# A decode step on one core: K cache turned by half units instead of quarters, with fewer VectorE instructions around it

## The chip, the core and the metric

The kernel runs on one core of a Trainium2 chip. The core has engines that run side by side: TensorE (PE, matmuls; PEld is its weight load), VectorE (DVE), ScalarE (ACT), GpSimd (POOL) and SyncE (SP), which here only issues DMAs. They order themselves by semaphores. The metric is the device time of one execution in microseconds, lower is better; the time before is a median of three runs.

## What is computed

Two sequences (B = 2) take one decode step each. A gate g = sigmoid(sum(x * gate_w)) mixes an attention block over a cache with a small dense block:

```
q = (x @ wq)                      x: 2 x 512, wq: 512 x 4096 (32 heads of 128)
p = softmax(q . K / sqrt(128))    K, V: 2 x 32 heads x 4096 keys x 128, bf16
a = (p . V) @ wo                  wo: 4096 x 512
b = relu(x @ w1) @ w2             w1: 512 x 1376, w2: 1376 x 512
out = g * a + (1 - g) * b
```

K and V are 67 MB each; everything else together is about 11 MB.

## The kernel before, in words

**Storage.** K and V are each cut into 8 units of 8 heads (8.39 MB, 64 KB on each of 128 partitions). Three regions of SBUF (`kv[:, 0..2]`) hold units in turn. The order of units is written out by hand: k0 to k4, then v0, k5, v1, k6, v2, k7, then v3 to v7. Unit n goes to region n mod 3, and after v7 the region of v5 takes wo and w2. wq, w1, x, gate_w and a 128x128 identity lie in region 2 at first, ahead of k2.

**DMA.** SP issues all large loads in that order from one queue (lines 216 to 239). Ahead of each it waits on the semaphore that says that the unit which last used the region is read: `pe_sc_u` for a K unit (its last score matmul), `pe_v_u` for a V unit. k2 instead waits for `pe_h`, `dve_setup` and `dve_q`, since it overwrites the small weights. ACT issues the two tiny loads of x and gate_w.

**Opening.** POOL builds constants (`constants`). `gate` turns x and gate_w by PE, copies them out of PSUM by VectorE, multiplies and sums them there, and spreads the sum to all partitions by a float32 matmul with ones; ACT takes the exponent, VectorE finishes g and 1 - g. `setup` reduces the identity to several masks. `q_proj` makes q, VectorE turns it into `q_sb`, and ACT writes it into the weight tiles `wz` (`w_block`). `ffn_h` makes h on PE in 11 blocks of w1's columns (the last of 96), and four VectorE instructions apply ReLU and the factor 1 - g.

**A K unit.** The keys land as rows. `k_turn` (L360) transposes the region in place on VectorE in 32x32 blocks of 32-bit words, in four instructions of 4096 words per partition. `k_scores` then runs 64 matmuls of 512 columns on PE, 16 for each of these quarters; of each four only the first loads weights (L393), the other three keep them (L365, a helper's line). The first matmul of a quarter waits for its turn `dve_kt_u_rp`. Scores of a whole batch (four K units) gather in four PSUM banks.

**Softmax.** After k3 (batch 0) and k7 (batch 1): `sm_max` on VectorE (maximum, then small turns), `sm_exp` on ACT, `sm_turn` on VectorE (turns the exponents E). `spread` on POOL multiplies E with a mask into the weights `ptm` for one V unit. `o_denominator` sums the exponents by four tiny matmuls and takes the reciprocal on VectorE.

**A V unit.** `v_unit`: 64 matmuls of 512 columns. `v_extract`: two VectorE instructions (L455, L459) reduce the result. `v_gather`: a small matmul adds it to the unit's batch.

**Order of work.** Each engine runs its list in the order in which the program adds to it (end of the kernel function): k0 to k3, softmax of batch 0, k4, then for v = 0 to 2 the V unit followed by one K unit, softmax of batch 1 after k7, and the rest of the V units. VectorE's list is thus: turns of k0 to k3, `sm_max(0)`, `sm_turn(0)`, turns of k4, extract of v0, turns of k5, and so on. At the end `o_scale`, `o_place`, and `project`, in which wo and w2 are multiplied as they land; VectorE and ACT cast the result and SP stores it.

Of the kernel before, what the change touches and what calls it, by code (L numbers as in the profile page):

```python
# [4 lines left out]
ALU = mybir.AluOpType  # L5
# [79 lines left out]
def bass_gated_mix__gqa_block_cached__dense_activation_relu__decode_kernel(  # L85
# [22 lines left out]
    id2 = sb("id2", [2, 2], bf16)  # L108
    xT = sb("xT", [128, 4, 2], bf16)
    xT32 = sb("xT32", [128, 4, 32], bf16)  # L110
    gwT = sb("gwT", [128, 4], bf16)
    xg = sb("xg", [128, 4, 2], f32)
    xgs = sb("xgs", [128, 2], f32)
# [27 lines left out]
    x_sb = kv[0:2, C, 21888:22400]  # L141
    gw_sb = kv[0:1, C, 22400:22912]
    ident = kv[:, C, 22912:23168].bitcast(f32)
    ones = kv[:, C, 23168:23424].bitcast(f32)
# [69 lines left out]
    act(lambda e: e.dma_start(x_sb, A_x.rearrange("b s d -> (b s) d")).then_inc(sem["x"], 16))  # L214
    act(lambda e: e.dma_start(gw_sb, gate_w.rearrange("(o d) -> o d", o=1)).then_inc(sem["gw"], 16))
# [20 lines left out]
    sp(lambda e: e.dma_start(w2_sb[0:96, 10, :], B_w2[1280:1376, :]).then_inc(sem["w2a"], 16))  # L236
    W2 = (("w2b", 0, 5, 0), ("w2c", 640, 4, 5), ("w2d", 1152, 1, 9))
    for name, row, n, r0 in W2:
        sp(lambda e, name=name, row=row, n=n, r0=r0: e.dma_start(
            w2_sb[:, r0:r0 + n, :].rearrange("p r n -> p (r n)"),  # L240
            B_w2[row:row + 128 * n, :].rearrange("(p r) n -> p (r n)", p=128)).then_inc(sem[name], 16))
# [4 lines left out]
    def constants():  # L246
        pool(lambda g: g.memset(id2[:], 0.0), signal="c_idz")
        pool(lambda g: g.affine_select(out=id2[:], in_=id2[:], pattern=[[-1, 2]], compare_op=ALU.not_equal, fill=1.0,
                                       base=0, channel_multiplier=1), waits=["c_idz"], signal="c_id2")
        pool(lambda g: g.memset(ones, 1.0), signal="c_ones")  # L250
        pool(lambda g: g.memset(ident, 0.0), signal="c_i0")
        pool(lambda g: g.affine_select(out=ident, in_=ident, pattern=[[-1, 128]], compare_op=ALU.not_equal, fill=1.0,
                                       base=0, channel_multiplier=1), waits=["c_i0"], signal="c_ident")
        pool(lambda g: g.memset(xT32[:], 0.0), signal="c_x32")
        for i in range(2):
            pool(lambda g, i=i: g.memset(wz[:, i], 0.0), signal=("c_wz" if i else None))
        pool(lambda g: g.memset(mpad[:], 0.0), signal="c_mpad")
        pool(lambda g: g.memset(selx[:], 0.0), signal="c_selx")
        for i in range(2):
            pool(lambda g, i=i: g.memset(sell[:, i], 0.0), signal=("c_sell" if i else None))  # L260
        pool(lambda g: g.memset(srow[:], 0.0), signal="c_s0")
        pool(lambda g: g.affine_select(out=srow[:], in_=srow[:], pattern=[[-1, 263]], compare_op=ALU.not_equal, fill=1.0,
                                       base=7, channel_multiplier=8), waits=["c_s0"], signal="c_srow")

    def setup():
        dve(lambda v: v.tensor_reduce(out=maskc[:], in_=ident.rearrange("p (t c h) -> p c t h", t=4, c=4), axis=AX.XY, op=ALU.add),
            waits=["c_ident"])
        dve(lambda v: v.tensor_reduce(out=mmax[:], in_=ident.rearrange("p (h x) -> p h x", h=8), axis=AX.X, op=ALU.add),
            signal="dve_m8")
        dve(lambda v: v.tensor_copy(out=mask8[:], in_=mmax[:]), waits=["dve_m8"], signal="dve_mask8")  # L270
# [8 lines left out]
    def gate():  # L279
        for t in range(4):  # L280
            pe(lambda e, t=t: e.transpose(PSB[0:128, XT_B0 + 2 * t:XT_B0 + 2 * t + 2], x_sb[:, t::4], id2[0:2, 0:2]),
               waits=(["c_id2"] if t == 0 else []), dwaits=([(sem["x"], 16)] if t == 0 else []))
        for t in range(4):
            pe(lambda e, t=t: e.transpose(PSB[0:128, XT_B0 + 8 + 2 * t:XT_B0 + 9 + 2 * t], gw_sb[:, t::4], id2[0:1, 0:1]),  # L284
               dwaits=([(sem["gw"], 16)] if t == 0 else []), signal=("pe_xT" if t == 3 else None))
        dve(lambda v: v.tensor_copy(out=xT[:], in_=PSB[0:128, XT_B0:XT_B0 + 8].rearrange("p (t b) -> p t b", t=4)),  # L286
            waits=["pe_xT"], signal="dve_xT0")
        dve(lambda v: v.tensor_copy(out=xT32[:, :, 0:2], in_=PSB[0:128, XT_B0:XT_B0 + 8].rearrange("p (t b) -> p t b", t=4)),
            waits=["c_x32"], signal="dve_x32")
        dve(lambda v: v.tensor_copy(out=gwT[:], in_=PSB[0:128, XT_B0 + 8:XT_B0 + 16:2]), signal="dve_xT")  # L290
        dve(lambda v: v.tensor_tensor(out=xg[:], in0=xT[:], in1=gwT[:].unsqueeze(2).to_broadcast([128, 4, 2]), op=ALU.mult),
            waits=["dve_xT"], signal="dve_xg")
        dve(lambda v: v.tensor_reduce(out=xgs[:], in_=xg[:].rearrange("p t b -> p b t"), axis=AX.X, op=ALU.add),
            waits=["dve_xg"], signal="dve_xgs")
        pe(lambda e: e.matmul(psf(0, 128, G_C0, 2), lhsT=ones, rhs=xgs[:, :], start=True, stop=True),
           waits=["dve_xgs", "c_ones"], signal="pe_z")
# [10 lines left out]
    def q_proj():  # L307
        wqv = wq_sb.rearrange("p (t u a x) -> p t a u x", t=4, u=4, a=4)
        for half in range(2):
            for t in range(4):  # L310
                for a in range(4):
                    pe(lambda e, half=half, t=t, a=a: e.matmul(  # L312
                        psf(32 * a, 32 * a + 32, V_C0 + BANK * half, BANK), lhsT=xT32[:, t, :],
                        rhs=wqv[:, t, a, 2 * half:2 * half + 2, :], start=(t == 0), stop=(t == 3), tile_position=(0, 32 * a)),
                       dwaits=([(sem["wq"], 16)] if half == 0 and t == 0 and a == 0 else []),
                       waits=(["dve_xT0", "dve_x32"] if half == 0 and t == 0 and a == 0 else []),
                       signal=("pe_q" if half == 1 and t == 3 and a == 3 else None))
# [8 lines left out]
    def ffn_h():  # L326
        for ft in range(11):
            m = 128 if ft < 10 else 96
            for t in range(4):
                def fn(e, ft=ft, t=t, m=m):  # L330
                    o = t * DFF
                    cols = w1_sb[:, o + 1280:o + 1376]
                    for _, row, n, r0 in W2:
                        if r0 <= ft < r0 + n:
                            cols = w1_sb[:, o + row + ft - r0:o + row + 128 * n:n]
                    return e.matmul(psf(0, m, H_C0 + 2 * ft, 2), lhsT=cols, rhs=xT[:, t, :], start=(t == 0), stop=(t == 3))
                pe(fn, dwaits=([(sem["w1"], 16)] if ft == 0 and t == 0 else []),
                   signal=("pe_h" if ft == 10 and t == 3 else None))
        for b in range(2):
            dve(lambda v, b=b: v.tensor_scalar(out=hT[:, 0:10, b], in0=PSF[:, H_C0 + b:H_C0 + 20:2], scalar1=0.0,  # L340
                                               scalar2=gm[:, b:b + 1], op0=ALU.max, op1=ALU.mult),
                waits=["pe_h", "dve_gm"])
            dve(lambda v, b=b: v.tensor_scalar(out=hT[0:96, 10, b:b + 1], in0=psf(0, 96, H_C0 + 20 + b, 1), scalar1=0.0,
                                               scalar2=gm[0:96, b:b + 1], op0=ALU.max, op1=ALU.mult),
                signal=f"dve_h{b}")
# [10 lines left out]
    def k_turn(u):  # L356
        what = ("k", u)
        reg = kv[:, reg_of(what), :].bitcast(dt.uint32)
        for rp in range(4):
            dve(lambda v, rp=rp: v.transpose(out=reg[:, 4096 * rp:4096 * (rp + 1)], in_=reg[:, 4096 * rp:4096 * (rp + 1)]),  # L360
                dwaits=([landed(what)] if rp == 0 else []), signal=f"dve_kt_{u}_{rp}")
# [8 lines left out]
    def k_scores(u):  # L370
        b, ub = divmod(u, 4)
        keys = kv[:, reg_of(("k", u)), :].rearrange("p (r j q e) -> p r j q e", j=2, q=32, e=2)
        for rp in range(4):
            pos = 8 * ub + 2 * rp
            for blk in range(4):
                j, e_ = divmod(blk, 2)
                for rb in range(4):
                    rc = 4 * rp + rb
                    waits = []
                    if blk == 0 and rb == 0:  # L380
                        waits = [f"dve_kt_{u}_{rp}"]
# [16 lines left out]
    def sm_max(b):  # L398
        dve(lambda v: v.tensor_reduce(out=mpad[:, 0:2], in_=PSF[:, 0:2048].rearrange("p (x h q) -> p h x q", h=2, q=16),  # L399
                                      axis=AX.XY, op=ALU.max),  # L400
            waits=[f"pe_sc_{4 * b + 3}", "c_mpad"] + ([f"dve_mt{b - 1}"] if b else []), signal=f"dve_m{b}")
# [51 lines left out]
    def v_extract(v):  # L453
# [4 lines left out]
            waits=[f"pe_v_{v}"] + ([f"dve_y_{v - 1}"] if v else []), signal=f"dve_x_{v}")  # L458
        dve(lambda e: e.tensor_reduce(out=X3[:], in_=X2[:].rearrange("p (c d) -> p d c", c=4), axis=AX.X, op=ALU.add),  # L459
            waits=[f"dve_x_{v}"] + ([f"pe_g_{v - 1}"] if v else []), signal=f"dve_y_{v}")  # L460
# [7 lines left out]
    def o_denominator(b):  # L468
        for h in range(2):
            pe(lambda e, h=h: e.matmul(psf(0, 32, L_C0 + b, 1), lhsT=sell[:, h, :], rhs=lsum[:, b, h:h + 1],  # L470
                                       start=(h == 0), stop=(h == 1), skip_group_check=True),
               waits=([f"act_exp{b}", "dve_setup", "dve_h1"] if h == 0 else []), signal=(f"pe_l{b}" if h else None))
        dve(lambda v: v.reciprocal(out=rinv[:, b:b + 1], in_=psf(0, 32, L_C0 + b, 1)), waits=[f"pe_l{b}"], signal=f"dve_rinv{b}")

    def o_scale(b):
        dve(lambda v: v.tensor_scalar(out=O_sb[:, b, :], in0=psf(0, 32, O_C0, 128), scalar1=rinv[:, b:b + 1],
                                      scalar2=gb[0:32, b:b + 1], op0=ALU.mult, op1=ALU.mult),
            waits=[f"pe_g_{4 * b + 3}", f"dve_rinv{b}", "dve_g"], signal=f"dve_O{b}")
# [54 lines left out]
    o_denominator(0)  # L533
    w_block(6)
    for v in range(8):
        v_unit(v)
        v_extract(v)
# [13 lines left out]
        if v == 3:  # L551
            o_denominator(1)
# [37 lines left out]
```

## Time and profile before

| quantity | value |
|---|---|
| time, median of 3 runs | 344.62 us (344.28 to 344.64) |
| the profiled execution's own time | 344.46 us |
| its span, first to last instruction | 343.1 us |
| busy: PE / VectorE / ACT / POOL | 179.8 / 169.7 / 13.5 / 35.5 us |
| mean granted TensorE clock | 0.781 of full speed |
| read from HBM | 145.43 MB, 424 GB/s over the span |
| VectorE's K turns (L360) | 32, 139.3 us in all, 4.41 us each |
| score matmuls (L393 and L365) | 128 and 384, 52.9 and 114.0 us |

How to read it: busy times are of one execution; engines overlap, so they don't add up to the span. A row of the time line gives start, duration, engine, line and operation, and in brackets the idle time ahead of it with what ended it. A busy PE counts pipelined matmuls, so its share says little of its speed; the granted clock (0.50 or 1.00 in most windows) says how fast it could go. DMA share above 1.0 in a short window is an effect of how packets are stamped.

### The profile page before, as it was taken

What the parts mean: (1) busy time and instruction counts of PE and PEld (TensorE: products, weight loads), DVE (VectorE), ACT (ScalarE), POOL (GpSimd) and SP (SyncE); (2) the same over time, 40 slices, a digit from 0 to 9 for tenths busy, and PEclk for the clock granted to TensorE, in tenths of its full rate; (3) what the DMA queues carried; (4) which work ended last, traced back from release to release, by engine and by line L of the source; (5) the groups of instructions that cost most, each with busy time, mean ns of one, the idle gap of its engine ahead of it and who ended that gap; (6) DMA issues with size and microseconds to landing.
All of it is one profiled execution on the core that took longest, in us unless ns stands there. A gap on an engine that the chain in (4) does not pass through costs nothing.

```text
span 343.1 us, 2541 instructions
## 1 busy us (share of the span) xinstructions
PE 179.8 (52%) x1322; PEld 39.6 (12%) x938; DVE 169.7 (49%) x87; ACT 13.5 (4%) x44; POOL 35.5 (10%) x50
## 2 busy tenths in 40 slices
PE   0510196996869409935980099205970503307353
PEld 0210000100001000120120011100020201102122
DVE  0210797979899489439910694219935020102020
ACT  1010001000010110000000000000020000000000
POOL 3000000000000040040013000400004040403100
PEclk9965599899989957995995579955996575856586
DMA  8998989999999989898999989999999999999995
GB/s 325 451 483 374 481 374 481 397 458 420 435 460 390 489 382 474 382 468 390 466 466 391 481 384 466 405 451 405 460 405 443 466 392 474 413 401 449 395 428 216
DMA packets 3588, 145.59 MB, mean 424 GB/s; under 512 B 405, under 2 KB 634, under 8 KB 890
## 3 DMA queue, kind: packets, MB, share of 16 engines
q1 hardware_dynamic: 3572, 145.43, 98.5%
q8 instruction: 9, 0.15, 0.2%
q10 hardware_dynamic: 6, 0.00, 0.0%
q14 instruction: 1, 0.01, 0.0%
HBM read 145.43 MB, written 0.00 MB: 424 GB/s over the span
## 4 chain that ended last, share of the span: by engine, by line
DMA 57%; DVE 24%; PE 9%; issue 4%; another core or an unknown queue 3%; SPq 1%; ACT 1%
DMA kv<-in_A_k_cache_dram 34%; DVE kv L360 22%; DMA kv<-in_B_w_dram 13%; DMA kv<-in_A_v_cache_dram 11%; PE PS L365 4%; PE PS L448 4%; PE PS L393 2%; DVE E L422 1%; ACT E L414 1%; DVE mpad L399 1%; DVE X L459 0%; SPq L232 0%; DVE X L455 0%; PE PS L500 0%
## 5 line engine op out<-in xcount | busy, mean ns | idle before, releaser
L360 DVE STREAM_TRANSPOSE kv<-kv 128x4096 uint32<-128x4096 uint32 x32 | 139.3, 4412 | 50.2 <-DMA kv<-in_A_k_cache_dram 50.2
L365 PE MATMUL PS<-kv,wz 128*128 128x512 bf16 x384 | 114.0, 407 | 0.0
L393 PE MATMUL PS<-kv,wz 128*128 128x512 bf16 x128 | 52.9, 413 | 94.5 <-DVE kv L360 94.4
L431 POOL TENSOR_TENSOR ptm<-E,mask 128x512 bf16<-128x512 bf16 x32 | 32.2, 1039 | 282.2 <-DVE E L422 158.5
L448 PE MATMUL PS<-kv,ptm 128*32 128x512 bf16 x512 | 38.6, 462 | 36.3 <-DMA kv<-in_A_v_cache_dram 36.3
L455 DVE TENSOR_TENSOR X<-PS,maskc 128x512 f32<-128x512 f32 x8 | 5.5, 687 | 79.4 <-PE PS L448 79.4
L393 PEld LDWEIGHTS PS<-kv,wz 128*128 128x128 bf16 x128 | 13.0, 102 | 206.2 <-DVE kv L360 120.6
L448 PEld LDWEIGHTS PS<-kv,ptm 128*32 128x32 bf16 x512 | 17.5, 113 | 54.3 <-issue 47.2
L351 ACT ACTIVATE wz<-q_sb 32x8 bf16<-32x8 bf16 x32 | 6.9, 214 | 154.5 <-PE PS L365 145.6
L464 PE MATMUL PS<-X,selx 128*32 128x128 f32 x16 | 3.5, 302 | 13.3 <-DVE X L459 13.3
L459 DVE TENSOR_REDUCE X<-X 128x128 f32<-128x512 f32 x8 | 8.2, 1024 | 0.3
L399 DVE TENSOR_REDUCE mpad<-PS 128x2 f32<-128x2048 f32 x2 | 4.6, 2292 | 7.5 <-PE PS L365 7.5
L414 ACT ACTIVATE E<-PS,negm 128x1024 bf16<-128x1024 f32 x4 | 4.4, 1109 | 81.8 <-DVE negm L410 81.8
L422 DVE STREAM_TRANSPOSE E<-E 128x2048 bf16<-128x2048 bf16 x2 | 4.6, 2312 | 4.7 <-ACT E L414 4.7
L312 PE MATMUL PS<-kv,xT 128*32 128x512 bf16 x32 | 3.6, 629 | 3.6 <-DMA kv<-in_A_wq_dram 3.6
L500 PE MATMUL PS<-kv,oW 128*2 128x128 bf16 x128 | 2.9, 264 | 4.5 <-DMA kv<-in_A_wo_dram 4.5
L510 DVE CAST ptm<-PS 2x128 bf16<-2x128 f32 x2 | 0.6, 280 | 9.1 <-PE PS L500 9.1
L319 DVE STREAM_TRANSPOSE ptm<-PS 128x1024 f32<-128x1024 f32 x1 | 1.3, 1251 | 6.3 <-PE PS L312 6.3
L286 DVE COPY xT<-PS 128x8 bf16<-128x8 bf16 x1 | 0.2, 164 | 8.1 <-PE PS L284 8.1
L510 ACT ACTIVATE ptm<-PS 2x128 bf16<-2x128 f32 x2 | 0.5, 270 | 84.0 <-PE PS L500 84.0
L464 PEld LDWEIGHTS PS<-X,selx 128*32 128x32 f32 x16 | 1.1, 112 | 19.0 <-DVE X L459 15.7
L500 PEld LDWEIGHTS PS<-kv,oW 128*2 128x2 bf16 x128 | 2.5, 102 | 4.8 <-DMA kv<-in_A_wo_dram 4.2
(56 smaller groups left out, 24.2 us busy)
## 6 DMA issues: line engine op xcount, KB each, us to landing
kv<-in_A_v_cache_dram SPq DMA_DIRECT2D x1, 6144.0 KB, 47.8
kv<-in_A_wq_dram SPq DMA_DIRECT2D x1, 4096.0 KB, 12.2
kv<-in_A_wo_dram SPq DMA_DIRECT2D x2, 2048.0 KB, 40.1
kv<-in_A_v_cache_dram SPq DMA_DIRECT2D x1, 2048.0 KB, 52.3
kv<-in_B_w_dram SPq DMA_DIRECT2D x1, 1376.0 KB, 15.0
kv<-in_B_w_dram SPq DMA_DIRECT2D x1, 640.0 KB, 43.4
kv<-in_B_w_dram SPq DMA_DIRECT2D x1, 512.0 KB, 44.2
kv<-in_A_k_cache_dram SPq DMA_DIRECT2D x8, 40.2
```

The source lines that it names most:

```text
L351: act(lambda e, a=a: e.activation(out=wz[32 * a:32 * a + 32, u % 2, :, 31 + 32 * a:33 + 32 * a], in_=q_sb[32 * a:32 * a + 32, b, ub].rearr ...
L360: dve(lambda v, rp=rp: v.transpose(out=reg[:, 4096 * rp:4096 * (rp + 1)], in_=reg[:, 4096 * rp:4096 * (rp + 1)]), dwaits=([landed(what)] i ...
L365: return e.add_instruction(mybir.InstMatmult(name=nc.get_next_instruction_name(), engine=mybir.EngineType.PE, ins=[e.lower_ap(rhs), e.lowe ...
L393: return e.matmul(dst, lhsT=w, rhs=m, start=first, stop=final, skip_group_check=True)
L399: dve(lambda v: v.tensor_reduce(out=mpad[:, 0:2], in_=PSF[:, 0:2048].rearrange("p (x h q) -> p h x q", h=2, q=16), axis=AX.XY, op=ALU.max) ...
L414: act(lambda a, h=h: a.activation(out=E[:].rearrange("p (x h q) -> p h x q", h=2, q=16)[:, h], in_=PSF[:, 0:2048].rearrange("p (x h q) -> ...
L422: dve(lambda v: v.transpose(out=E[:], in_=E[:]), waits=[f"act_exp{b}"], signal=f"dve_et{b}")
L431: pool(lambda g, src=src, dst=dst: g.tensor_tensor(out=dst, in0=src, in1=msk, op=ALU.mult), waits=([f"dve_et{b}", "dve_mask8"] + ([f"pe_v_ ...
L448: pe(lambda e, ci=ci, t=t: e.matmul(psf(32 * t, 32 * t + 32, c0, 512), lhsT=ptm[:, ci].rearrange("p c h -> p (c h)"), rhs=rows[:, 512 * ci ...
L455: dve(lambda e: e.tensor_tensor(out=X2[:].rearrange("p (c d) -> p c d", c=4), in0=psf(0, 128, c0, 512).rearrange("p (c d) -> p c d", c=4), ...
L459: dve(lambda e: e.tensor_reduce(out=X3[:], in_=X2[:].rearrange("p (c d) -> p d c", c=4), axis=AX.X, op=ALU.add), waits=[f"dve_x_{v}"] + ([ ...
L500: pe(lambda e, t=t, n=n, w=w, m=m: e.matmul(psf(32 * t, 32 * t + 2, FIN_C0, 128), lhsT=w, rhs=m[:, 128 * t:128 * t + 128], start=(n == 0), ...
```

## The change

Nothing of the arithmetic on K and V changes. The edits are:

- K is turned in two instructions of 8192 words per partition instead of four of 4096, and PE waits for halves (`rp % 2 == 0`).
- Gate: x and gate_w lie in one tile of 3 rows and are turned together; one copy brings them to `xT32`; the product and the sum are made by four matmuls with gate_w's column, broadcast, as weights. The tiles `xT`, `gwT`, `xg`, `xgs` and `ones` go.
- Setup: `mask8` is made by one reduction (maximum) instead of a reduction and a cast.
- h: 11 blocks of 128 columns (the block that was 96 wide reads 32 columns more than are used), and two VectorE instructions instead of four. The block of 96 rows of w2 is now the first 96 rows; the DMAs keep their sizes and order.
- The denominators of both batches are made together, after v3's matmuls, with one reciprocal; those of batch 0 stood ahead of v0's matmuls.
- Waits that follow from others are left out (`c_mpad`, `dve_mt`, `dve_y`, `pe_g`, `dve_rinv`, `dve_g`), and POOL makes its constants in another order.

```diff
     def k_turn(u):
         what = ("k", u)
         reg = kv[:, reg_of(what), :].bitcast(dt.uint32)
-        for rp in range(4):
-            dve(lambda v, rp=rp: v.transpose(out=reg[:, 4096 * rp:4096 * (rp + 1)], in_=reg[:, 4096 * rp:4096 * (rp + 1)]),
-                dwaits=([landed(what)] if rp == 0 else []), signal=f"dve_kt_{u}_{rp}")
+        for h in range(2):
+            dve(lambda v, h=h: v.transpose(out=reg[:, 8192 * h:8192 * (h + 1)], in_=reg[:, 8192 * h:8192 * (h + 1)]),
+                dwaits=([landed(what)] if h == 0 else []), signal=f"dve_kt_{u}_{h}")
...
-                    if blk == 0 and rb == 0:
-                        waits = [f"dve_kt_{u}_{rp}"]
+                    if blk == 0 and rb == 0 and rp % 2 == 0:
+                        waits = [f"dve_kt_{u}_{rp // 2}"]
...
-            pe(lambda e, t=t: e.transpose(PSB[0:128, XT_B0 + 2 * t:XT_B0 + 2 * t + 2], x_sb[:, t::4], id2[0:2, 0:2]),
-               waits=(["c_id2"] if t == 0 else []), dwaits=([(sem["x"], 16)] if t == 0 else []))
+            pe(lambda e, t=t: e.transpose(PSB[0:128, XT_B0 + 4 * t:XT_B0 + 4 * t + 3], x_sb[:, t::4], id3[0:3, 0:3]),
+               waits=(["c_id3"] if t == 0 else []), dwaits=([(sem["x"], 16), (sem["gw"], 16)] if t == 0 else []),
+               signal=("pe_xT" if t == 3 else None))
+        dve(lambda v: v.tensor_copy(out=xT32[:, :, 0:3], in_=PSB[0:128, XT_B0:XT_B0 + 16].rearrange("p (t b) -> p t b", t=4)[:, :, 0:3]),
+            waits=["pe_xT"], signal="dve_xT")
...
-        pe(lambda e: e.matmul(psf(0, 128, G_C0, 2), lhsT=ones, rhs=xgs[:, :], start=True, stop=True),
-           waits=["dve_xgs", "c_ones"], signal="pe_z")
+            pe(lambda e, t=t: e.matmul(psf(0, 128, G_C0, 2), lhsT=xT32[:, t, 2:3].to_broadcast([128, 128]), rhs=xT32[:, t, 0:2],
+                                       start=(t == 0), stop=(t == 3)),
+               waits=(["dve_xT"] if t == 0 else []), signal=("pe_z" if t == 3 else None))
...
-            dve(lambda v, b=b: v.tensor_scalar(out=hT[:, 0:10, b], in0=PSF[:, H_C0 + b:H_C0 + 20:2], scalar1=0.0,
+            dve(lambda v, b=b: v.tensor_scalar(out=hT[:, :, b], in0=PSF[:, H_C0 + b:H_C0 + 2 * NF:2], scalar1=0.0,
                                                scalar2=gm[:, b:b + 1], op0=ALU.max, op1=ALU.mult),
-                waits=["pe_h", "dve_gm"])
-            dve(lambda v, b=b: v.tensor_scalar(out=hT[0:96, 10, b:b + 1], in0=psf(0, 96, H_C0 + 20 + b, 1), scalar1=0.0,
-                                               scalar2=gm[0:96, b:b + 1], op0=ALU.max, op1=ALU.mult),
-                signal=f"dve_h{b}")
+                waits=["pe_h"] + ([] if b else ["dve_gm"]), signal=f"dve_h{b}")
...
-            waits=[f"pe_v_{v}"] + ([f"dve_y_{v - 1}"] if v else []), signal=f"dve_x_{v}")
+            waits=[f"pe_v_{v}"], signal=f"dve_x_{v}")
...
     k_scores(4)
-    o_denominator(0)
     w_block(6)
     for v in range(8):
         v_unit(v)
+        if v == 3:
+            o_denominator()
         v_extract(v)
```

## The prediction

> **What bounds the kernel now.** I read the page's slices first, then the time line of VectorE and of SP's queue, then the chain of waits, then windows of 2 us.
>
> The page's DMA rows, 40 slices of 8.6 us each (share of the 16 DMA engines in tenths, then GB/s):
>
> ```profile
> DMA  8998989999999989898999989999999999999995
> GB/s 325 451 483 374 481 374 481 397 458 420 435 460 390 489 382 474 382 468 390 466 466 391 481 384 466 405 451 405 460 405 443 466 392 474 413 401 449 395 428 216
> ```
>
> No slice between the first and the last is empty. The exact rate comes from VectorE's time line (start us, us, what):
>
> ```profile
> 94.96 17.42 DVE L360 STREAM_TRANSPOSE kv<-kv 128x4096 uint32<-128x4096 uint32 x4 [1.96 <-DMA kv<-in_A_k_cache_dram]
> ...
> 123.95 17.38 DVE L360 STREAM_TRANSPOSE kv<-kv 128x4096 uint32<-128x4096 uint32 x4
> ...
> 153.41 17.42 DVE L360 STREAM_TRANSPOSE kv<-kv 128x4096 uint32<-128x4096 uint32 x4 [2.87 <-DMA kv<-in_A_k_cache_dram]
> ```
>
> A K turn that was released by a DMA starts when its unit lands. Those starts are 36.87, 56.22, 75.58, 94.96 (k0 to k3), 153.41 (k5), 191.96 (k6) and 230.66 (k7); the chain has v5 at 288.70. Each difference, divided by the transfers in it (1, 1, 1, 3, 2, 2, 3), is 19.3 to 19.5 us for 8.39 MB, some 433 GB/s, with VectorE busy or not. So one queue streams without a hole from start to end, the last transfer (w2) lands at 340.66, and 2.4 us of work follow. **The time is that of the stream**: an edit counts only if it makes a transfer be issued after the one ahead of it has run out, or changes the start or the 2.4 us at the end.
>
> So the quantity to read is the lead of each issue: the landing of the transfer ahead less the moment of issue. SP's time line gives the issues:
>
> ```profile
> 116.12 0.33 SPq L229 DMA_DIRECT2D kv<-in_A_k_cache_dram  x1
> 145.06 0.33 SPq L229 DMA_DIRECT2D kv<-in_A_v_cache_dram  x1
> 148.78 0.33 SPq L229 DMA_DIRECT2D kv<-in_A_k_cache_dram  x1
> 174.78 0.33 SPq L229 DMA_DIRECT2D kv<-in_A_v_cache_dram  x1
> ```
>
> These are k5, v1, k6 and v2. With landings from above, or issue plus time to landing from the DMA view, the leads are 17.6 us for k3, k4, v0 and k5; **8.35 for v1** (k5 lands at 153.41); 23.8 for k6 (v1 lands at 145.06 + 27.5); 17.2 for v2; 32.7 for k7; 17.5 for v3 and v5; about 33 for v4, v6, v7 and wo. The lead of 8.35 costs nothing: v1 lands 19.15 us after k5.
>
> How a K unit frees its region is seen in the chain (start, us, what):
>
> ```profile
> 94.96 0.04 DVE kv L360
> 95.00 4.33 issue
> 99.33 13.06 DVE kv L360 x3
> 112.40 0.05 issue
> 112.44 0.39 PE PS L393
> 112.83 0.65 PE PS L365 x3
> 113.48 0.22 PE PS L393
> ...
> 116.10 0.02 issue
> 116.12 2.30 DVE mpad L399
> ```
>
> Four turns last 17.4 us; PE starts the last quarter's 16 matmuls 0.05 us later and needs 3.67 us (four groups of 0.87 and 0.2 of drain). From landing to free: 21.16 us.
>
> **The change, part by part.**
>
> Turns: 32 instructions of 4.41 us become 16. The trace has no 8192 columns. Below: the 128x1024 turn (L319) took 1.25, so a column is (4.412 - 1.251)/3072 = 1.029 ns and a half 8.63. Above: twice 4.41 = 8.82. I take 8.71, between them and near two start-to-start steps of 4.33. A unit's turns then last 17.4 as before (17.3 to 17.6); the saving in instructions is worth at most 0.1 us each time.
>
> What changes is the tail. PE waits for whole halves: after the last turn it has 32 matmuls, 8 x 0.87 + 0.2 = 7.14 us in place of 3.67. Landing to free becomes 17.40 + 0.05 + 7.14 = 24.59, **3.43 us later**. For k0 to k3 the next unit's turn does not wait for that, so nothing adds up: leads of 17.6 become 14.2. PE's first half must be done by then: 8.71 + 0.05 + 6.94 = 15.70 at full clock, inside 17.40.
>
> At k4 it adds up twice. k3's scores end at 119.55 in place of 116.12; maximum, exponent and the turn of E (7.8 us, unchanged) follow, so k4's turn starts at 127.38 in place of 123.95. There PE is cold. The windows (us, busy and count of PE, PEld, DVE, ACT, POOL, clock, DMA share, GB/s):
>
> ```profile
> 128.00:130.00 2.00, 1.59 (x4) 0.25 (x2) 2.00 (x2) 0.00 (x0) 0.14 (x1) 0.50 1.21 524
> 130.00:132.00 2.00, 2.00 (x6) 0.14 (x1) 2.00 (x1) 0.00 (x0) 0.00 (x0) 0.50 1.14 492
> 132.00:134.00 2.00, 2.00 (x9) 0.19 (x2) 2.00 (x2) 0.00 (x0) 0.00 (x0) 0.78 0.23 98
> ```
>
> PE started k4 at 128.35 and the granted clock stayed 0.50 until 132.9 (0.78 is 0.44 of the window at 0.50): 4.5 us cold, half of it lost. The same reading gives 2.7 us (k0), 5.7 (k5), 4.7 (k6), 3.6 (k7). In the quarter scheme the other quarters absorb that; now the first half ends at 127.38 + 15.70 + half the cold stretch, and the second can't start before 144.83. For the five stretches in the order k0, k4, k5, k6, k7, k4's scores end at 151.97, 152.47, 153.07, 152.57 and 152.02; middle **152.4 in place of 145.06**. v1's lead falls from 8.35 to between 0.3 and 1.4 us.
>
> [...]
>
> How much lead does an issue need? SP issues the first DMA at 0.74, and in windows of 0.2 us the first bytes move in 1.60 to 1.80: 0.95 us. At the end the last bytes move before 340.60 and PE is released at 340.66, so k5's last bytes are at about 153.3. v1's bytes could start at 152.92, 153.42, 154.02, 153.52 and 152.97: the slowest queue is dry for 0, 0.12, 0.72, 0.22 and 0 us, **mean 0.21**. Whether a restarted queue also needs time to ramp, no row shows in mid-stream. Bounds: nothing (a later transfer starts with a full packet on each engine), and 2.9 us, by which the stretch before k0 is late (14.0 MB at 433 GB/s are 32.3 us from 1.7; k0 landed at 36.87). That stretch holds small and strided weight transfers, so I take a value near nothing.
>
> [...]
>
> Behind k4 nothing is short. v0's matmuls end at about 156.0 and its extract on VectorE at 157.8, so k5's turn starts 4.4 us late and its scores end near 183: v2's lead is 9. k6 waits for its landing (191.96) and the lateness is back to 3.4: leads of 14 (v3, v5). After k7 the softmax is 3.4 later, POOL's spread for v4 ends at 267.4 in place of 263.9, and v4 lands at 269.3: still covered, by 1.9; without that cover v7's issue would move, and it has 33.
>
> The rest costs nothing, by its cover. Gate: five small DVE instructions (8.14 to 8.83) and a float32 matmul become one copy and four 128x128 matmuls of 2 columns (0.17 each by L336); all of it ends by 10.5, PE's next work waits for wq at 13.03. The transposes now wait for gw too, which DVE's first copy did already (8.14). setup, h: three instructions of 0.2 us fewer before 19, DVE is then idle until 36.87; k2's issue near 18.35 has a lead of 38. The longer w1 load of the last block is as the other 40. POOL's constants end by 4.5. Denominators: four small matmuls leave PE's queue ahead of v0 (about 0.15 us, inside the doubt about T) and stand behind v3's; there they wait for the exponent of batch 1 (near 261) ahead of the gather, which waits for VectorE's extract behind it anyway. No wait is added otherwise; the ones left out never ended last in the list of waits. The DMAs are as many and as large, in the same order, and the end is untouched.
>
> **Sum.** Against the profiled execution (344.46 us: span 343.1 and 1.36 around it; 0.16 under the median): plus 0.21 on the stream. On the median 344.62 that is 344.8.
>
> **Rivals.** 0.2% (0.69 us) is about what a measurement of this kernel can tell from no change.
> 1. Covered or nearly so (forecast): 344.4 to 345.3, likeliest 344.8. For it: every other lead stays above 9, and the stream has no other master. 58%.
> 2. The queue runs dry ahead of v1 by enough to see. It decides from the end of k4's scores at 153.04 with no ramp (153.3 - 0.95 + 0.69), or with the middle 152.4 from a ramp of 0.65. Price 0.7 to 3.6 us (0.72 + 2.9 at most), likeliest 1: 345.6. For it: the doubled tail counts twice on exactly the issue with the least lead. Against: the lead only just ends. 36%, with the half turn that costs its upper 8.82 and so doesn't do what it promises (0.4 later at k4, 345.0 to 345.6).
> 3. Faster: the shorter opening moves the stream's start forward, of whose 2.9 us of lateness a part could be its own (343.6 if a third goes). Against: SP's first three issues wait for nothing on VectorE. 6%.
> The range takes in case 1, most of 2 and the near part of 3: 344.2 to 347.0.
>
> **What would show it.** Right: 16 turns of 8.6 to 8.8 us; K scores freed 24.6 after landing; v1 issued at 152 to 153, k6's turn starting within 0.7 us of 191.96, and the landings shifted by one constant from v1 on. Wrong: later landings before k5, a K turn far from 8.7, or dry slices elsewhere. If k6's turn starts over 1 us late, case 2 holds and its size is the ramp; if all landings are earlier, case 3.

## The result and the profile after

The changed kernel takes **347.66 us** (median of 4 runs, 347.17 to 348.19) against 344.56 before: ratio 1.0092, 95% interval 1.0071 to 1.0113. It is 3.1 us slower. I had forecast 344.8, with 347.0 as the upper end. The profiled execution took 347.17 us, its span is 345.9.

VectorE's time line after (start us, us, what), the rows that answer to those shown of before:

```profile
95.13 17.30 DVE L341 STREAM_TRANSPOSE kv<-kv 128x8192 uint32<-128x8192 uint32 x2 [2.04 <-DMA kv<-in_A_k_cache_dram]
...
127.49 17.26 DVE L341 STREAM_TRANSPOSE kv<-kv 128x8192 uint32<-128x8192 uint32 x2
...
157.21 17.30 DVE L341 STREAM_TRANSPOSE kv<-kv 128x8192 uint32<-128x8192 uint32 x2
...
194.36 17.30 DVE L341 STREAM_TRANSPOSE kv<-kv 128x8192 uint32<-128x8192 uint32 x2 [6.80 <-DMA kv<-in_A_k_cache_dram]
233.09 17.30 DVE L341 STREAM_TRANSPOSE kv<-kv 128x8192 uint32<-128x8192 uint32 x2 [8.18 <-DMA kv<-in_A_k_cache_dram]
```

k3 still lands at 95.13 (94.96 before), so up to there the stream is as it was. k6 lands at 194.36 in place of 191.96, 2.4 us late, k7 at 233.09 in place of 230.66, 2.4 late, and the store of the output is issued at 344.68 in place of 341.98, 2.7 late. One loss, between k3 and k6, is carried almost unchanged to the end. SP's time line says where:

```profile
119.66 0.33 SPq L223 DMA_DIRECT2D kv<-in_A_k_cache_dram  x1
151.95 0.33 SPq L223 DMA_DIRECT2D kv<-in_A_v_cache_dram  x1
155.54 0.33 SPq L223 DMA_DIRECT2D kv<-in_A_k_cache_dram  x1
181.99 0.33 SPq L223 DMA_DIRECT2D kv<-in_A_v_cache_dram  x1
```

v1 is issued at 151.95 in place of 145.06. By the DMA view k5 lands at 119.66 + 33.5 = 153.16, so v1's lead is 1.2 us, and still DMA engines stood idle. Windows of 1 us (columns as in the prediction; the last two are DMA share and GB/s), first before:

```profile
150.00:151.00 1.00, 0.00 (x0) 0.00 (x0) 0.54 (x1) 0.00 (x0) 1.00 (x2) 1.00 0.45 197
151.00:152.00 1.00, 0.00 (x0) 0.00 (x0) 0.00 (x0) 0.00 (x0) 1.00 (x2) 1.00 1.88 803
152.00:153.00 1.00, 0.00 (x0) 0.00 (x0) 0.00 (x0) 0.00 (x0) 0.93 (x1) 1.00 0.49 197
153.00:154.00 1.00, 0.00 (x0) 0.00 (x0) 0.59 (x1) 0.00 (x0) 0.00 (x0) 0.68 1.96 852
```

and after:

```profile
150.00:151.00 1.00, 1.00 (x6) 0.10 (x1) 0.00 (x0) 0.00 (x0) 0.00 (x0) 1.00 0.31 131
151.00:152.00 1.00, 1.00 (x9) 0.12 (x8) 0.00 (x0) 0.04 (x1) 0.00 (x0) 1.00 0.00 0
152.00:153.00 1.00, 1.00 (x24) 0.48 (x20) 0.00 (x0) 0.83 (x4) 0.00 (x0) 1.00 0.81 262
153.00:154.00 1.00, 1.00 (x24) 0.48 (x20) 0.00 (x0) 0.00 (x0) 0.00 (x0) 1.00 2.26 786
154.00:155.00 1.00, 1.00 (x24) 0.53 (x20) 0.00 (x0) 0.00 (x0) 0.00 (x0) 1.00 0.00 0
```

A window books a packet's time and bytes at the moment at which the packet starts: the share reaches 2.26 above. In both traces the median packet of 64 KB takes 2.42 us, and most engines start theirs together (before, 13 of 16 start v1 between 150.94 and 151.40), so the bytes come in lumps, and an empty window alone shows no idle engine. Before, a lump falls in 151 to 152: v1's first packets. After, it is missing and comes at 153. Most engines had run out of work about two microseconds ahead of the landing that I had measured the lead against; the last of the experiments' sections shows it engine by engine.

The chain of waits after, at k3 (start, us, what), shows the other half of the mechanism:

```profile
95.13 8.72 DVE kv L341
...
104.29 0.65 PE PS L346 x3
105.16 1.24 PE PS L346 x3
106.41 0.43 PE PS L374
106.83 1.28 PE PS L346 x3
...
119.67 2.30 DVE mpad L380
```

From the first half on the chain runs through PE: three matmuls take 1.28 us while the granted clock is 0.50 (windows from 106 to 108) and 0.65 at 1.00 (110 to 114). The low clock holds PE's first half until 112.70, a little past the end of the second turn at 112.43. From landing to free it is now 119.67 - 95.13 = 24.54 us (21.16 before).

### The profile page after: what moved, and what is told of

Read it like the earlier page. It is cut to its first block, busy times and chain, and to the rows that moved or that the text cites. A ratio compares the mean times of both kernels' runs of the same rounds, so it can differ in the third digit from the quotient of the medians.

```text
span 345.9 us, 2492 instructions
## 1 busy us (share of the span) xinstructions
PE 180.2 (52%) x1320; PEld 38.4 (11%) x936; DVE 167.6 (48%) x63; ACT 13.5 (4%) x44; POOL 35.4 (10%) x50
## 4 chain that ended last, share of the span: by engine, by line
DMA 56%; PE 27%; DVE 15%; SPq 1%; ACT 1%; issue 0%
DMA kv<-in_A_k_cache_dram 33%; PE PS L346 17%; DMA kv<-in_B_w_dram 13%; DVE kv L341 13%; DMA kv<-in_A_v_cache_dram 10%; PE PS L374 6%; PE PS L429 4%; DVE E L403 1%; ACT E L395 1%; DVE mpad L380 1%; DVE X L440 0%; SPq L226 0%; PE PS L482 0%; DVE X L436 0%; DVE ptm L492 0%
## 5 line engine op out<-in xcount | busy, mean ns | idle before, releaser
L341 DVE STREAM_TRANSPOSE kv<-kv 128x8192 uint32<-128x8192 uint32 x16 | 138.4, 8688 | 39.5 <-DMA kv<-in_A_k_cache_dram 39.5
L346 PE MATMUL PS<-kv,wz 128*128 128x512 bf16 x384 | 116.1, 413 | 0.0
L374 PE MATMUL PS<-kv,wz 128*128 128x512 bf16 x128 | 53.7, 419 | 99.4 <-DVE kv L341 99.3
L429 PE MATMUL PS<-kv,ptm 128*32 128x512 bf16 x512 | 37.7, 455 | 34.2 <-DMA kv<-in_A_v_cache_dram 34.2
L429 PEld LDWEIGHTS PS<-kv,ptm 128*32 128x32 bf16 x512 | 16.3, 112 | 54.0 <-issue 45.4
L332 ACT ACTIVATE wz<-q_sb 32x8 bf16<-32x8 bf16 x32 | 6.9, 214 | 162.4 <-PE PS L346 152.8
L482 PE MATMUL PS<-kv,oW 128*2 128x128 bf16 x128 | 3.8, 308 | 3.6 <-DMA kv<-in_A_wo_dram 3.2
L482 PEld LDWEIGHTS PS<-kv,oW 128*2 128x2 bf16 x128 | 3.2, 120 | 3.9 <-DMA kv<-in_A_wo_dram 3.5
```

The source lines that it names most:

```text
L332: act(lambda e, a=a: e.activation(out=wz[32 * a:32 * a + 32, u % 2, :, 31 + 32 * a:33 + 32 * a], in_=q_sb[32 * a:32 * a + 32, b, ub].rearr ...
L341: dve(lambda v, h=h: v.transpose(out=reg[:, 8192 * h:8192 * (h + 1)], in_=reg[:, 8192 * h:8192 * (h + 1)]), dwaits=([landed(what)] if h == ...
L346: return e.add_instruction(mybir.InstMatmult(name=nc.get_next_instruction_name(), engine=mybir.EngineType.PE, ins=[e.lower_ap(rhs), e.lowe ...
L374: return e.matmul(dst, lhsT=w, rhs=m, start=first, stop=final, skip_group_check=True)
L429: pe(lambda e, ci=ci, t=t: e.matmul(psf(32 * t, 32 * t + 32, c0, 512), lhsT=ptm[:, ci].rearrange("p c h -> p (c h)"), rhs=rows[:, 512 * ci ...
L482: pe(lambda e, t=t, n=n, w=w, m=m: e.matmul(psf(32 * t, 32 * t + 2, FIN_C0, 128), lhsT=w, rhs=m[:, 128 * t:128 * t + 128], start=(n == 0), ...
```

## The experiments

**Theory A:** the half turns delay v1's issue twice over (k3's tail ahead of the softmax, k4's own), the queue runs dry ahead of v1, and nothing else counts. **Rivals:** the small edits cost it (B), or long turns slow the stream or shorter leads elsewhere cost (C, later G). A second question is how much lead an issue needs.

### The turns or the other edits?

before_halves is the kernel before with `k_turn` and the waits in `k_scores` taken from the change; after_quarters is the change with both taken back:

```diff
-        for rp in range(4):
-            dve(lambda v, rp=rp: v.transpose(out=reg[:, 4096 * rp:4096 * (rp + 1)], ...
+        for h in range(2):
+            dve(lambda v, h=h: v.transpose(out=reg[:, 8192 * h:8192 * (h + 1)], ...
```

> The kernel before with K turned by halves and nothing else of the change. Theory A (the queue runs dry ahead of v1): v1 issued near 152, k6 landing about 2.4 us later than in the kernel before, time 347 to 348.2 (ratio 1.007 to 1.011). Rival B (the small edits cost it: gate, h, denominators, constants): 344.3 to 344.9. Rival C (the stream itself is slower beside long turns): landings late already before k5, in proportion to the turns.

> The changed kernel with K turned by quarters again, all the other edits kept. Theory A: v1 issued near 145, no hole, 344.3 to 344.8 (ratio 0.999 to 1.001). Rival B: 347 or more.

before_halves: 347.99 us, ratio 1.0097 (1.0082 to 1.0112), v1 issued at 152.24, k6 at 194.95. after_quarters: 344.55, ratio 0.9999 (0.9990 to 1.0009), v1 issued at 145.30. The turns carry the whole loss; all the other edits together are worth nothing that can be measured. B falls.

### Which turns?

`TURNS` gives the number of turns of a unit, and `k_scores` waits to match. The lines are from after_k4_quarters; the others have {3: 4}, {3: 4, 4: 4}, and {3: 2, 4: 2} with a default of 4 (before_k34_halves):

```diff
+TURNS = {4: 4}
...
-        for h in range(2):
...
+        n = TURNS.get(u, 2)
+        w = 16384 // n
+        for h in range(n):
...
```

> The changed kernel with k4 alone turned by quarters; seven of eight units still by halves. Theory A: the tail ahead of v1 counts once instead of twice, v1 issued near 148.5, a lead of about 4.7 us; if an issue needs the 3.5 us that I read from the changed kernel's trace, no loss: 344.3 to 344.9. Rival C: seven eighths of the loss stay, 347.2. If the needed lead is larger than 5: 345 to 346.

> The changed kernel with k3 alone turned by quarters. Theory A: batch 0's softmax and k4's turn start 3.4 us earlier, v1 issued near 148.5 (up to 149.5 with a long cold stretch in k4), lead 3.7 to 4.7: 344.3 to 345. Rival C: 347.2. If only k4's own tail mattered: 347.

> The changed kernel with k3 and k4 turned by quarters, the other six units by halves. Theory A: only the two tails ahead of v1 cost, so v1 is issued near 145.1, lead 8.3, and no loss is left: 344.4 to 344.9. Rival G (half turns of other units cost too, by the DMA's rate or the shorter leads of 14 elsewhere): 345.2 to 347.

> The kernel before with only k3 and k4 turned by halves. Theory A: the whole loss, 347.2 to 348.2. Rival G: only a part, 345 to 346.5.

With both in quarters and the other six units in halves: 344.70 us, ratio 1.0000 (0.9990 to 1.0009). With only those two in halves: 348.02, ratio 1.0094 (1.0079 to 1.0109). SP's time line of after_k34_quarters, with v1's and k6's issue:

```profile
145.06 0.33 SPq L224 DMA_DIRECT2D kv<-in_A_v_cache_dram  x1
148.64 0.33 SPq L224 DMA_DIRECT2D kv<-in_A_k_cache_dram  x1
```

and of before_k34_halves:

```profile
152.50 0.33 SPq L230 DMA_DIRECT2D kv<-in_A_v_cache_dram  x1
156.21 0.33 SPq L230 DMA_DIRECT2D kv<-in_A_k_cache_dram  x1
```

Six half-turned units are free, two cost everything: theory A holds, C and G fall. With one of the two in quarters the loss is small and scattered: k4 alone 345.25 us (344.72 to 346.83), ratio 1.0028 (1.0014 to 1.0042); k3 alone 345.85 (344.50 to 347.16), ratio 1.0034 (1.0014 to 1.0053). I had expected at most 344.9 and 345.0. The two profiled executions, with leads of 4.6 and 4.0 us, are among the shorter ones (344.80 and 344.50); the longer ones have no trace, and whether their leads were shorter is not shown. That my figure of 3.5 for the needed lead was too small is shown by v1_after_v0 below, which lost 2 us with a lead of 4.4.

### How much lead does an issue need?

Here everything is as before the change, quarters too; only v1's issue is held back by one more wait on SP:

```diff
-            waits = [freed(order[n - NREG])]
+            waits = [freed(order[n - NREG])] + (["pe_v_0"] if what == ("v", 1) else [])
```

with `dve_x_0`, `dve_y_0` or `pool_pt1` in the other three, and a signal on matmul 32 or 48 of v0's 64 in the last two.

> The kernel before, quarters and all, but SP issues v1 only after v0's last matmul (near 148.8). Lead before k5's landing (153.4): 4.6 us. Theory A with a needed lead of 3.6 us (one packet in flight, 2.4, first byte 0.8 to 0.95, some rest): no loss, 344.3 to 344.8. Rival D (only the time to the first byte counts, 0.95, and the loss of the change has another cause): also no loss.

> As above, v1 issued after the first extract instruction of v0 (near 149.5), lead 3.9 us. Theory A: 344.3 to 344.9. Rival D: no loss.

> As above, v1 issued after the second extract instruction (near 150.55), lead 2.9 us. Theory A, loss growing linearly below 3.6: plus 0.7, 345.2. Theory A', a whole packet slot is lost at once: plus 2.4, 346.9. Rival D: no loss, 344.5.

> As above, v1 issued after POOL's spread for v1 (near 152.95), lead 0.5 us. Theory A: plus 3.1, 347.6. Theory A' in whole slots: plus 2.4 or 4.8. Rival D: plus 0.5, 345.0.

> The kernel before with quarters, v1 issued after half of v0's matmuls (near 146.9), lead 6.5 us. It looks for the point between the lead of 8.35 (no loss) and that of 4.4 (1.5 us lost). Theory P with two 64 KB packets in hand and the time to the first byte (4.85 + 0.8 = 5.65): no loss, 344.4 to 344.9. If three packets are in hand (8.1): about 1 us lost, 345.3 to 346.

> The kernel before with quarters, v1 issued after three quarters of v0's matmuls (48 of 64). The wait after 32 gave an issue at 147.61, lead 5.9, and no loss; the wait after 64 gave 148.64, lead 4.4, and 1.5 us of loss in the times. Lead here about 5.2. Theory H (the engines must have the next transfer some 4 us ahead of the landing: 2.4 from the last read to the landing, 0.9 from issue to first read, 0.6 at a restart): no loss, 344.4 to 344.9. If the need is nearer 5.5: 345 to 346.

The lead is k5's landing less v1's issue in the profiled execution. The loss in the stream is the time from k5's to k7's landing (four transfers) less the 77.25 us of before, by the times at which the trace has their semaphores complete; it leaves out what happens elsewhere. The column "profiled" is the time of that same execution; the last two columns are for the median of all runs, the ratio against the kernel before as timed beside them.

| kernel | lead us | loss, k5 to k7 | profiled us | median us | ratio (95%) |
|---|---|---|---|---|---|
| before | 8.3 | 0 | 344.46 | 344.56 | 1 |
| after_k34_quarters | 8.1 | 0.0 | 344.45 | 344.70 | 1.0000 (0.9990 to 1.0009) |
| v1_after_v0_half | 5.8 | 0.1 | 344.89 | 344.63 | 1.0000 (0.9991 to 1.0010) |
| v1_after_v0_3q | 5.3 | 0.6 | 345.29 | 344.79 | 1.0002 (0.9992 to 1.0012) |
| after_k4_quarters | 4.6 | 0.2 | 344.80 | 345.25 | 1.0028 (1.0014 to 1.0042) |
| v1_after_v0 | 4.4 | 0.7 | 346.42 | 346.25 | 1.0044 (1.0029 to 1.0059) |
| after_k3_quarters | 4.0 | 0.2 | 344.50 | 345.85 | 1.0034 (1.0014 to 1.0053) |
| v1_after_x0 | 3.5 | 1.2 | 346.04 | 346.37 | 1.0057 (1.0040 to 1.0074) |
| v1_after_y0 | 2.5 | 1.2 | 345.83 | 345.84 | 1.0034 (1.0021 to 1.0047) |
| after | 1.2 | 2.7 | 347.17 | 347.66 | 1.0092 (1.0071 to 1.0113) |
| before_halves | 0.8 | 3.4 | 347.50 | 347.99 | 1.0097 (1.0082 to 1.0112) |
| before_k34_halves | 0.6 | 3.1 | 347.56 | 348.02 | 1.0094 (1.0079 to 1.0109) |
| v1_after_pt1 | 0.2 | 3.5 | 348.45 | 348.18 | 1.0102 (1.0087 to 1.0117) |

From a lead of 2.5 us down, **the loss is 4 us less the lead, within 0.3**, whether half turns or a bare wait made the issue late: that is the whole mechanism in one line. From about 5.3 us up the median loses nothing. Rival D (only the 0.95 us to the first byte count) falls with v1_after_y0 and v1_after_pt1; A' (whole slots) falls too. Theory A's figure of 3.6 falls as well: v1_after_v0 and v1_after_x0 should have lost nothing and lost 1.5 and 1.7.

Between 3.5 and 5.3 us the loss is not a function of the lead alone. In v1_after_v0 v1's first packets follow k5's without a hole on most engines, but several take longer than 2.42 us, one of them 4.38. By k7 that is a loss of 0.7; another 1.5 us appear between v6's and v7's first landing (16.0 us in place of 14.5). These are one engine's: 15 engines finish that part of v7 by 322.92, the last at 324.42. At 313.28 the trace has a packet of 16 KB of the instruction queue (q8 on the page), 1.02 us long, exactly behind a packet of one of the two engines that were latest already. Before, such a packet at 313.15 left v7's landing in step. Why some first packets are stretched, no run isolates.

### What are the 4 us?

The next three load k5, or v1, or both, by four DMAs of 16 KB per partition in place of one of 64 KB, in the changed kernel; the reader waits for all four.

```diff
+        elif what in SPLIT:
+            for i in range(4):
+                sp(lambda e, n=n, what=what, i=i: e.dma_start(kv[:, n % NREG, 8192 * i:8192 * (i + 1)], unit_in(what)[:, 8192 * i:8192 * (i + 1)])
+                   .then_inc(sem_split[what] if i < 3 else sem_reg[n % NREG], 16), waits=(waits if i == 0 else []))
...
```

> The changed kernel, with k5 alone loaded by four DMAs of 16 KB per partition in place of one of 64 KB; same bytes, same place in the queue, k5's turn waits for all four. Theory P (an issue must come ahead of the landing by the packets that an engine has in hand, so the needed lead is a multiple of the packet time of the transfer ahead, 2.42 us for 64 KB, 0.6 for 16 KB): the lead of 1.2 us is nearly enough, loss 0 to 1 in place of 2.6 to 3.6: 344.6 to 345.7. Rival F (a fixed latency of about 3.5 to 5 us from issue to full rate, whatever the packets): 347.2 to 348.2 as in the changed kernel.

> The changed kernel, with v1 alone loaded by four DMAs of 16 KB per partition (v0's successor in the region, read after all four have landed). Theory P: the packet that counts is that of the transfer ahead (k5, 64 KB), so the hole stays, and only the 0.6 us of a first full packet may shrink: 346.6 to 348. Rival F: 347.2 to 348.2. If the size of the first packets after the restart sets the loss: 345 to 346.

> The changed kernel, with both k5 and v1 loaded by four DMAs of 16 KB per partition. Theory P: as with k5 alone or up to 0.6 better, 344.5 to 345.5. Rival F: 347.2 to 348.2. If four DMAs of smaller packets cost rate by themselves, it shows here twice against k5 alone.

| kernel | lead us | loss, k5 to k7 | profiled us | median us | ratio (95%) |
|---|---|---|---|---|---|
| after_k5_16k | 1.9 | 2.0 | 346.75 | 347.28 | 1.0078 (1.0057 to 1.0099) |
| after_v1_16k | 0.3 | 3.7 | 348.29 | 347.56 | 1.0080 (1.0063 to 1.0097) |
| after_k5_v1_16k | 0.2 | 3.9 | 348.43 | 348.25 | 1.0103 (1.0088 to 1.0118) |

All three lie on the same line, 4 us less the lead. Theory P, that the need follows the packet size, falls. F's total holds, but the records show that most of it is no latency of the issue.

A K or V load runs on 16 DMA engines, and on each of them the records end with a packet of 4 bytes. In the profile after, 0.43 to 0.51 us behind each of these the semaphore of k5's load goes up by one, and at 16 the load has landed. So the packets under 512 B tell when each engine is done. The DMA view of the profile after, for 150.6 to 151.5, 152.6 to 152.8 and 152.9 to 153.8:

```profile
DMA packets 14, 0.00 MB, mean 0 GB/s; under 512 B 14, under 2 KB 14, under 8 KB 14
...
DMA packets 2, 0.00 MB, mean 0 GB/s; under 512 B 2, under 2 KB 2, under 8 KB 2
...
DMA packets 16, 1.05 MB, mean 1165 GB/s; under 512 B 0, under 2 KB 0, under 8 KB 0
...
q1 hardware_dynamic: 16, 1.05, 340.9%
```

Fourteen engines are done with k5 between 150.75 and 151.43, the middle one of the sixteen at 150.9. Two are late, at 152.63 and 152.73, and the landing at 153.17 is theirs. Then the 16 first packets of v1 start, the middle one at 153.1, 1.1 us after the issue. They take 340.9% of 0.9 us, 3.07 us each in place of 2.42. So the 4 us are **2.3 from the middle engine's end to the landing, 1.1 from the issue to its next packet, and 0.7 by which the first packet after a halt is longer**. With a lead of 1.2 the middle engine stands idle for 2.2 us and loses some 0.7 more, 2.9 in all; by k7 the middle increment of the semaphore is 2.7 late.

The first of these terms is mostly the spread of the engines: in all 17 profiles 13 or 14 of the 16 finish k5 within 0.7 us of each other, and the middle one 1.9 to 2.4 us ahead of the landing. Why do the two late engines, done only 0.2 to 0.3 us before v1's first packets start, not decide? After the halt all 16 start within 0.9 us, so the old lateness is gone, and a new one builds up. The trace shows one source: at 158.62 a packet of the instruction queue takes 0.95 us and the data packet behind it 2.90. One engine then finishes v1 at 174.99, the other 15 by 173.73.

From the last engine's last bytes to the landing it is 0.4 to 0.7 us in all 17 profiles (152.73 to 153.17 in the profile after, 152.71 to 153.39 before).

## Why the prediction was wrong

- **Right: what bounds the kernel.** The turns of k1 to k3 start within 0.25 us of before, and only the lead of an issue counted. k0's turn starts at 35.80 in place of 36.87 and nothing comes of it: before, 15 engines finish k0 by 35.57 and one at 36.85; after, all by 35.78, and one engine is late from k1 on.
- **Right: the turns.** A half takes 8.69 us (8.71 forecast), landing to free 24.54 (24.59). That the second figure is so close is a little luck: at k3 PE's first half, at a low clock, ended 0.27 us after the second turn, and the sum had taken it as done by then.
- **Right: the double count.** v1's issue was forecast at 152.4 (151.97 to 153.07 by the cold stretch) and came at 151.95; in other kernels with k3 and k4 in halves it came between 151.54 and 152.96. v2's came at 181.99 (near 183), and leads elsewhere of 9 and more cost nothing, as six half-turned units show.
- **Right: the small edits at nothing** (after_quarters 0.9999).
- **Wrong, and it decided: "k5's last bytes are at about 153.3" and, from it, "the slowest queue is dry for 0, 0.12, 0.72, 0.22 and 0 us".** The sum took the landing for the end of the work on all engines. It is that of the slowest; the middle engine ended at 150.9. It was idle for 2.2 us where the sum had 0.21, and the first packet after the halt, which the sum put near nothing, cost some 0.7 more. My point of decision, an issue at 152.35, lies near 150. The 0.95 us from issue to first bytes was right (1.0 to 1.1).
- **The 0.1 us from last byte to landing was misread too.** 340.66 is the landing of the third piece of w2 (issued at 296.49, 44.2 us). The last bytes, before 340.60, are those of the fourth, issued at 296.96 and landed 44.0 us later, at about 341.0. So 0.4 us pass there as well.
- **Rival 2 was the case that came.** Its price (0.7 to 3.6) holds the 3.1 us; I gave it 36% and "likeliest 1". Its upper end was reached by luck: 2.9 us is the lateness ahead of k0, and 1.3 of it is the one late engine named above, not a restart.
- **The clock.** The four runs lie at 347.17, 347.20, 348.13 and 348.19. In the profile after, PE starts k4 at 136.22 and the granted clock stays 0.50 for 3.0 us more:

```profile
136.00:138.00 2.00, 1.78 (x5) 0.25 (x2) 2.00 (x2) 0.00 (x0) 0.00 (x0) 0.50 1.06 459
138.00:140.00 2.00, 2.00 (x8) 0.11 (x1) 2.00 (x1) 0.00 (x0) 0.00 (x0) 0.70 1.21 524
```

In after_v1_16k PE starts at 136.24 and the clock stays 0.50 for 5.2:

```profile
138.00:140.00 2.00, 2.00 (x6) 0.14 (x1) 2.00 (x1) 0.00 (x0) 0.00 (x0) 0.50 1.21 524
140.00:142.00 2.00, 2.00 (x7) 0.14 (x1) 2.00 (x1) 0.00 (x0) 0.00 (x0) 0.63 1.21 524
```

v1 is issued at 151.95 and 152.88. So with halves the length of this stretch reaches the time, a term that the prediction had. That it separates the two pairs of runs fits in size, but the other runs have no trace.

## What to carry to other kernels

In a kernel that one DMA queue bounds, list the lead of every issue and judge an edit by the smallest one, and count a delay as often as it stands on the path to that issue. A lead against the landing is not a lead against the engines, since the landing is that of the slowest of 16 and most are done earlier (here the middle one by 1.9 to 2.4 us): here a lead of 5.3 us cost the median nothing, and below 2.5 each microsecond of lateness cost one. Count the packets that end a load, engine by engine, before you trust a small lead. Fewer, longer instructions saved little here (a unit's turns took 17.30 us in place of 17.42) and lengthened the tail of the engine that waits for them (landing to free 24.54 in place of 21.16).

## What the runs showed of the hardware

- A load of 8.39 MB landed with the slowest of 16 DMA engines. For k5 the middle one was done 1.9 to 2.4 us earlier in all 17 profiles; the last engine's last bytes came 0.4 to 0.7 us ahead of the landing.
- After a halt of all 16 engines the first packets of 64 KB took 3.1 us in place of 2.42 (after), those of 16 KB some 1.15 in place of 0.61 (after_v1_16k).
- A packet of 16 KB of the instruction queue took its engine 0.95 us, and the data packet behind it 2.90 in place of 2.42 (158.62 in the profile after).
- Splitting a transfer of 64 KB per partition into four of 16 KB neither helped nor cost by itself: the losses of 2.0, 3.7 and 3.9 us, at leads of 1.9, 0.3 and 0.2, lie on the line of the unsplit transfers.
- The cold stretch of k4 (granted clock 0.50), with the same start of PE within 0.02 us of the span, lasted 3.0 us in one execution (after) and 5.2 in another (after_v1_16k).
